# Eight three-slice products of state and w_in in place of twelve two-slice ones, and another output tile last, in a fused attention and snake kernel

## The chip, the cores and the metric

The kernel runs on one core of a Trainium2 chip. The metric is the device time of one execution in microseconds (us); the number compared is the median of several executions. TensorE (PE in the profile) does the matrix products and writes them to PSUM, which has eight banks here; ScalarE (ACT), VectorE (DVE) and GpSimd (POOL) do the elementwise work; SyncE (SP) issues most of the transfers.

## The reference

Two things are computed one after the other. First, for eight batches and eight heads, tokens read from a small state and the state reads from the tokens. Then every row that comes out goes through a two-matrix network with a snake activation.

```python
B, H, S, Ns, D = 8, 8, 512, 32, 64           # x: B,H,S,D; state: B,H,Ns,D
a  = softmax(x @ state.T / sqrt(D))          # over the 32 state slots
xread = a @ state                            # (B, H, 512, 64)
a2 = softmax(state @ x.T / sqrt(D))          # over the 512 tokens
sread = a2 @ x                               # (B, H, 32, 64)
rows = concat([xread, sread], axis=2)        # 8 * 544 = 4352 rows of 512 = H*D
h = rows @ w_in                              # 512 -> 2048
g = h + sin(alpha * h) ** 2 / (alpha + 1e-9)
out = g @ w_out                              # 2048 -> 512, float32
```

## The kernel before

The 4352 rows are handled as nine groups: group t = 0 to 7 holds the 512 ordinary tokens of batch t, and group t = 8 holds the 256 state reads of all batches together. Every group has 16 slices f of 128 columns of the 2048-wide hidden layer, and output tiles of 128 rows: four for an ordinary group, two for the state group.

For an ordinary batch the kernel does not form `xread` and then multiply it by `w_in`. It multiplies the state by `w_in` first: M = state times w_in, a table of 128 rows (four heads of 32 slots) by 2048 columns, for two head groups g. The hidden layer is then the attention weights AT times M, two matmuls for each slice f. The product for M is cut into four slices s of 512 columns. One slice takes eight matmuls which each use only a 64 by 32 piece of the array (`m`, L489), into two PSUM banks, one for each g. `me` (L497) copies a bank to M in SBUF as bf16; it runs on ACT or DVE. Slice s of M serves the hidden slices f = 4s to 4s+3.

The steps are small functions, and the string ORDER calls them one by one. Each engine works strictly in the order in which its own instructions stand there, so ORDER is the schedule, and it also names the PSUM bank of every product. The steps that matter here are:

- `lx`, `pk`, `td`: load x of a batch (POOL's queue), repack it (DVE), transpose it by DMA (SP's queue). `sc`, `ex`: the scores and their exponential. `rs`, `rr`, `nm`: row sums, reciprocals, normalised weights A (on POOL). `ad` (L441): the DMA transpose from A to AT, on SP's queue.
- `w` (L451), `cs` (L462), `rc`, `xs`: the state's read of a batch. The matmuls of `cs` use 64 columns of the array.
- `m` and `me`: the state times w_in, as above. `h` (L538, and L544 for the state group) and `hg` (L553): the hidden slice.
- `si` (L561), `sq` (L202 on POOL or DVE, L570 on ACT), `gt` (L577, DVE): sine, square, and the snake sum gT, which frees the bank of `h`.
- `o.t.st.f0.f1` (L588): matmuls f0 to f1 of an output tile; sixteen make a tile. `oc` (L596) copies the bank out, `os` (L603, or L606 for group 8) stores it on SP's queue. `oh`, `och` and `osh` are the same for a tile that is cut in 384 and 128 columns; the last tile is.

Before the change, M of batches 2 to 7 is made in twelve steps `m` of two slices, and each of them holds four banks. Batches 0 and 1 have eight slices at the start that are placed one or two at a time. The pool of M has two buffers. The tile that stands last in ORDER is the first one of the state group, `oh.8.0.0` and `oh.8.0.1`, right after `o.8.1`. Its store goes through this address pattern, whose outer dimension is the batch:

```python
ov = k.out.rearrange("(b t) c -> b t c", t=k.TB)
k.nc.sync.dma_start(ov[:, k.S + st::2, cols], o_sb[:, cols])
```

An ordinary tile is stored as 128 rows at a fixed step:

```python
k.nc.sync.dma_start(k.out[r0:r0 + k.C * (k.P - 1) + 1:k.C, cols], o_sb[:, cols])
```

Of the kernel before, what the change touches and what calls it, by code (L numbers as in the profile page):

```python
# [32 lines left out]
m.0.1.6.4 si.0.1 m.1.1.0.7 hg.0.3.0.2 me.1.1.1.A sq.0.2.V hg.0.3.1 sq.0.1.G me.1.1.0.V si.0.0  # L33
warm_up.2.128.7 gt.0.2 warm_up.2.128.7 me.0.1.1.A warm_up.2.128.0 sq.0.0.G warm_up.2.128.7
warm_up.2.128.0 me.0.1.0.A gt.0.1 m.1.2.7.1 si.0.3 m.0.2.4.0 hg.0.4.0.6 me.1.2.1.V me.1.2.0.A
hg.0.4.1 sq.0.3.G hg.0.6.0.5 me.0.2.0.V hg.0.6.1 si.0.4 hg.0.5.0.1 hg.0.5.1 me.0.2.1.V si.0.6
hg.0.11.0.7 sq.0.4.G hg.0.7.0.4 gt.0.0 hg.0.7.1 si.0.5 hg.0.11.1 hg.0.8.0.0 gt.0.3 hg.0.8.1 sq.0.6.A
sq.0.5.G o.0.0.0.2.3 si.0.11 gt.0.4 o.0.0.2.3 o.0.3.0.2.2 si.0.7 o.0.3.2.3 gt.0.6 sq.0.11.G
o.0.3.3.4 o.0.2.0.1.6 si.0.8 o.0.2.1.2 gt.0.5 o.0.3.4.5 sq.0.7.A o.0.2.2.3 sq.0.8.G o.0.2.3.4
gt.0.11 hg.0.9.0.5 hg.0.9.1 hg.0.10.0.1 gt.0.7 hg.0.10.1 si.0.9 o.0.2.4.6 gt.0.8 si.0.10 o.0.3.5.6  # L40
sq.0.9.G o.0.0.3.4 o.0.3.6.8 sq.0.10.A xt.1.1.7 pk.1.1.V pk.1.0.V xt.1.0.4 xc.1.1.1.A xc.1.1.0.V
o.0.0.4.5 gt.0.10 xc.1.0.1.A o.0.0.5.6 sc.1.1.0 xc.1.0.0.A o.0.0.6.7 gt.0.9 o.0.2.6.8 sc.1.0.7
m.0.3.1.4 ex.1.0 o.0.1.0.1.5 me.0.3.0.V o.0.1.1.4 me.0.3.1.V o.0.1.4.7 hg.0.13.0.1 o.0.1.7.8 ex.1.1
rs.1.0 hg.0.13.1 hg.0.12.0.4 o.0.2.8.9 si.0.13 rr.1.0 hg.0.12.1 rs.1.1 nm.1.0.0.4.G m.1.3.7.0
o.0.3.8.9 rr.1.1 o.0.3.9.10 me.1.3.1.V o.0.3.10.11 nm.1.1.0.4.G o.0.1.8.10 me.1.3.0.V si.0.12
o.0.1.10.12 o.0.0.7.8 sq.0.13.G ad.1 hg.0.15.0.0 sq.0.12.A o.0.0.8.9 hg.0.15.1 o.0.0.9.10 gt.0.12
o.0.0.10.11 si.0.15 hg.0.14.0.7 o.0.0.11.12 gt.0.13 hg.0.14.1 sq.0.15.A o.0.1.12.13 o.0.2.9.11
si.0.14 gt.0.15 o.0.3.11.14 sq.0.14.A o.0.0.12.13 pk.2.0.V o.0.1.13.14 pk.2.1.V h.1.2.4 gt.0.14
h.1.4.1 td.2 si.1.2 lx.3.0.1 h.1.0.0 si.1.4 o.0.0.13.15 sq.1.2.V h.1.1.7 si.1.0 gt.1.2 sq.1.4.G
o.0.3.14.16 si.1.1 o.0.2.11.13 sq.1.0.A oc.0.3.V h.1.3.4 sq.1.1.G gt.1.4 o.0.0.15.16 os.0.3 h.1.6.2  # L50
si.1.3 oc.0.0.V o.0.2.13.15 si.1.6 sq.1.3.G o.0.2.15.16 gt.1.1 h.1.13.1 os.0.0 oc.0.2.A o.0.1.14.15
gt.1.0 o.0.1.15.16 sq.1.6.G si.1.13 h.1.7.3 os.0.2 gt.1.3 oc.0.1.A h.1.5.7 sq.1.13.G h.1.15.6 si.1.7
gt.1.6 os.0.1 o.1.1.0.1.0 si.1.5 o.1.1.1.3 sq.1.7.G gt.1.13 o.1.1.3.4 si.1.15 h.1.8.5 h.1.9.4
sq.1.5.A sq.1.15.G gt.1.7 o.1.2.0.1.2 si.1.8 h.1.12.1 gt.1.5 o.1.2.1.2 si.1.9 o.1.2.2.3 sq.1.8.G
o.1.2.3.4 gt.1.15 h.1.10.3 si.1.12 o.1.2.4.5 sq.1.9.A pk.3.1.V o.1.2.5.6 sq.1.12.G gt.1.8 h.1.11.7
si.1.10 h.1.14.6 gt.1.9 o.1.1.4.5 si.1.11 sq.1.10.G o.1.2.6.7 sc.2.1.5 gt.1.12 si.1.14 o.1.2.7.9
o.1.1.5.6 sq.1.11.A pk.3.0.V o.1.1.6.7 sq.1.14.G gt.1.10 o.1.1.7.8 td.3 sc.2.0.4 o.1.3.0.1.1 gt.1.11
o.1.3.1.2 ex.2.0 o.1.1.8.10 gt.1.14 o.1.3.2.3 o.1.2.9.10 o.1.3.3.5 o.1.1.10.11 o.1.2.10.11 ex.2.1
o.1.2.11.12 rs.2.0 o.1.2.12.15 rr.2.0 o.1.2.15.16 rs.2.1 nm.2.0.0.4.G m.2.2.3.7.6.4 oc.1.2.A
o.1.3.5.6 rr.2.1 me.2.2.0.A me.2.2.1.V w.0.5 os.1.2 nm.2.1.0.4.G me.2.3.1.A o.1.3.6.7 me.2.3.0.V  # L60
cs.0 m.2.0.2.3.7.4 ad.2 rc.0 o.1.3.7.8 me.2.1.1.A o.1.3.8.9 sc.3.0.6 me.2.0.1.V me.2.1.0.A
o.1.3.9.11 me.2.0.0.A sc.3.1.4 xs.0.0 o.1.1.11.12 xs.0.1 o.1.1.12.13 ex.3.0 o.1.1.13.15 o.1.3.11.12
ex.3.1 rs.3.0 o.1.3.12.14 o.1.1.15.16 rr.3.0 h.2.0.3 rs.3.1 nm.3.0.0.4.G oc.1.1.A o.1.3.14.16 si.2.0
rr.3.1 h.2.9.7 os.1.1 nm.3.1.0.4.G oc.1.3.V o.1.0.0.1.2 h.2.2.5 os.1.3 h.2.1.6 lx.4.0.1 ad.3 h.2.3.4
si.2.9 o.1.0.1.3 sq.2.0.V si.2.1 o.1.0.3.4 sq.2.9.G gt.2.0 o.1.0.4.6 si.2.3 o.1.0.6.8 si.2.2
sq.2.1.G h.2.8.0 gt.2.9 h.2.4.1 sq.2.3.A o.2.3.0.1.3 sq.2.2.G o.1.0.8.9 gt.2.1 si.2.8 h.2.5.7 si.2.4
o.1.0.9.10 gt.2.3 o.1.0.10.11 sq.2.8.G o.1.0.11.12 si.2.5 h.2.7.6 gt.2.2 o.2.3.1.2 sq.2.4.A
o.1.0.12.13 sq.2.5.G gt.2.8 o.1.0.13.14 si.2.7 o.1.0.14.15 h.2.6.4 gt.2.4 h.2.14.5 sq.2.7.A gt.2.5
o.1.0.15.16 o.2.3.2.3 si.2.6 o.2.3.3.4 pk.4.0.V o.2.3.4.5 oc.1.0.A pk.4.1.V h.2.11.0 sq.2.6.G gt.2.7
si.2.14 h.2.12.1 td.4 h.2.10.7 si.2.11 sq.2.14.G o.2.0.0.1.2 gt.2.6 o.2.0.1.2 si.2.10 o.2.0.2.4  # L70
sq.2.11.A o.2.0.4.5 os.1.0 sq.2.10.V o.2.0.5.6 gt.2.14 h.2.15.6 si.2.12 o.2.3.5.6 gt.2.10 h.2.13.4
si.2.15 sq.2.12.G o.2.0.6.7 gt.2.11 o.2.3.6.7 si.2.13 o.2.3.7.9 sq.2.15.G o.2.3.9.10 gt.2.12
sq.2.13.A o.2.0.7.10 gt.2.13 o.2.0.10.11 sc.4.1.5 sc.4.0.7 gt.2.15 o.2.3.10.12 ex.4.0 o.2.3.12.13
o.2.0.11.12 w.1.0 cs.1 o.2.3.13.14 rc.1 o.2.3.14.15 ex.4.1 o.2.3.15.16 m.3.0.1.4.6.7 oc.2.3.A rs.4.0
o.2.0.12.13 me.3.0.1.A o.2.0.13.14 os.2.3 o.2.0.14.15 me.3.0.0.V me.3.1.1.A o.2.0.15.16 o.2.1.0.2.5
rr.4.0 oc.2.0.A rs.4.1 o.2.1.2.3 nm.4.0.0.4.G o.2.1.3.4 me.3.1.0.A h.3.1.3 os.2.0 rr.4.1 xs.1.1
m.3.2.4.1.7.2 si.3.1 nm.4.1.0.4.G xs.1.0 h.3.0.6 me.3.3.1.V h.3.2.0 ad.4 me.3.3.0.V o.2.1.4.6
lx.5.0.1 h.3.6.2 me.3.2.1.V si.3.2 o.2.2.0.2.7 sq.3.1.V si.3.0 o.2.2.2.3 sq.3.2.G me.3.2.0.V
h.3.14.1 si.3.6 o.2.2.3.4 gt.3.1 o.2.2.4.5 si.3.14 sq.3.0.G o.2.2.5.7 gt.3.2 o.2.2.7.8 sq.3.6.A
o.2.2.8.9 h.3.9.4 sq.3.14.G gt.3.0 h.3.8.3 si.3.9 gt.3.6 h.3.5.0 si.3.8 h.3.10.6 sq.3.9.G gt.3.14  # L80
o.2.2.9.10 si.3.5 o.2.2.10.13 si.3.10 sq.3.8.G gt.3.9 h.3.15.2 sq.3.5.A o.2.2.13.14 h.3.7.1
sq.3.10.G gt.3.8 si.3.15 o.2.2.14.15 o.2.1.6.7 h.3.4.4 si.3.7 gt.3.5 sq.3.15.G o.2.2.15.16 o.2.1.7.8
si.3.4 gt.3.10 o.2.1.8.10 sq.3.7.A o.2.1.10.11 gt.3.15 sq.3.4.G o.2.1.11.13 oc.2.2.A o.2.1.13.14
gt.3.7 o.2.1.14.16 os.2.2 h.3.12.3 gt.3.4 oc.2.1.A h.3.3.0 si.3.12 pk.5.0.V o.3.3.0.1.6 os.2.1
m.4.2.2.7.1.5 pk.5.1.V si.3.3 sq.3.12.V td.5 o.3.3.1.2 me.4.2.1.V me.4.3.1.A o.3.3.2.3 sq.3.3.G
o.3.2.0.1.4 me.4.3.0.A o.3.2.1.2 gt.3.12 o.3.2.2.3 h.3.11.5 me.4.2.0.A gt.3.3 h.4.12.7 si.3.11
h.4.9.1 si.4.12 h.4.10.3 sq.3.11.V o.3.3.3.4 si.4.9 gt.3.11 h.4.11.2 sq.4.12.G o.3.2.3.4 si.4.10
o.3.2.4.6 sq.4.9.A o.3.2.6.7 gt.4.12 sq.4.10.G o.3.2.7.9 si.4.11 o.3.2.9.10 gt.4.9 o.3.2.10.11
o.3.3.4.5 sq.4.11.A o.3.3.5.6 gt.4.10 o.3.3.6.8 m.4.0.0.5.7.1 gt.4.11 o.3.3.8.9 me.4.1.0.A
me.4.0.1.V h.3.13.3 me.4.0.0.A h.4.8.2 me.4.1.1.V h.4.15.7 si.3.13 h.4.2.5 si.4.8 sq.3.13.V  # L90
o.3.1.0.2.0 lx.6.0.1 si.4.15 gt.3.13 h.4.1.1 o.3.3.9.10 si.4.2 o.3.3.10.11 sq.4.15.V o.3.1.2.3
sq.4.8.G si.4.1 gt.4.15 o.3.1.3.4 o.3.3.11.13 sq.4.2.A h.4.13.3 sq.4.1.G gt.4.8 o.3.3.13.14 h.4.3.7
si.4.13 gt.4.2 o.3.2.11.12 o.3.3.14.15 si.4.3 sq.4.13.G o.3.3.15.16 gt.4.1 h.4.5.2 oc.3.3.A h.4.6.5
sq.4.3.G si.4.5 gt.4.13 o.3.2.12.13 os.3.3 o.3.0.0.1.1 si.4.6 h.4.14.6 sq.4.5.G o.3.2.13.14 gt.4.3
h.4.4.3 si.4.14 o.3.0.1.2 sq.4.6.A o.3.0.2.3 sq.4.14.G gt.4.5 o.3.0.3.4 h.4.0.7 si.4.4 gt.4.6
o.3.0.4.5 o.3.1.4.5 si.4.0 sq.4.4.G o.3.1.5.6 gt.4.14 w.2.2 sq.4.0.A o.3.2.14.16 pk.6.1.V o.3.1.6.7
gt.4.4 h.4.7.5 oc.3.2.A sc.5.0.6 pk.6.0.V os.3.2 si.4.7 o.3.1.7.8 gt.4.0 sc.5.1.4 td.6 o.3.0.5.7
ex.5.0 sq.4.7.G o.3.1.8.9 o.3.0.7.11 gt.4.7 o.3.0.11.12 o.3.1.9.10 o.3.0.12.13 o.3.1.10.11 ex.5.1
rs.5.0 cs.2 m.5.0.3.7.5.6 rs.5.1 o.4.3.0.1.4 me.5.1.1.A o.4.3.1.2 rr.5.0 o.3.1.11.12 me.5.0.1.V
me.5.1.0.A o.3.1.12.13 nm.5.0.0.4.G o.3.1.13.14 o.3.0.13.14 me.5.0.0.A rr.5.1 rc.2 o.3.0.14.16  # L100
nm.5.1.0.4.G o.4.3.2.4 oc.3.0.A m.6.0.6.5.7.3 xs.2.0 xs.2.1 os.3.0 o.4.3.4.5 me.6.0.1.A me.6.0.0.V
ad.5 o.4.3.5.6 sc.6.0.1 me.6.1.1.A sc.6.1.2 me.6.1.0.V o.3.1.14.15 w.3.5 ex.6.0 o.3.1.15.16 ex.6.1
rs.6.0 o.4.0.0.1.6 o.4.3.6.7 cs.3 oc.3.1.A rs.6.1 m.5.2.3.7.1.2 os.3.1 o.4.3.7.8 rr.6.0 me.5.3.1.A
me.5.2.1.V o.4.3.8.9 nm.6.0.0.4.G o.4.3.9.10 me.5.2.0.A o.4.2.0.1.0 rr.6.1 o.4.3.10.11 rc.3
# [560 lines left out]
```

## Time and profile before

| what | value |
|---|---|
| median of 3 runs | 225.24 us (225.04 to 225.65) |
| the profiled execution | 226.94 us |
| its span in the trace | 225.2 us |
| PE busy | 213.6 us, 95% |
| ACT, DVE, POOL busy | 173.4, 162.3, 112.3 us |
| matmuls of the output product, L588, 128x512 | 511, mean 379 ns (they overlap; one starts about every 216 ns) |
| matmuls of state times w_in, L489 | 256, mean 382 ns |
| copies of M, L497 | 34 on ACT of 593 ns, 30 on DVE of 678 ns |

The profiled execution took 1.74 us more than its span, and 1.70 us more than the median of the runs. In the rows of the profile a name such as `o_ps<-w_out_sb,gT` is output and inputs, `x14` a count, and brackets hold the idle time before an instruction and what ended it. A busy time of PE is modelled, since matmuls are pipelined.

### The profile page before, as it was taken

The numbers are of one execution on the slowest core, as the hardware profiler recorded it, in microseconds if no ns is written. First come the engines' busy times: TensorE is split into PE (matmuls) and PEld (weight loads), VectorE is DVE, ScalarE is ACT, GpSimd is POOL, SyncE is SP. The second block draws the span as 40 slices with busy tenths as digits, with TensorE's granted clock in tenths as the row PEclk, the third lists the DMA queues.
The fourth block names the chain that finished last, engine by engine and source line by source line (L and its number), as shares of the span: only waits on it lengthen the run. The fifth ranks groups of instructions, "written<-read, shape, count | busy, mean of one in ns | idle before, by whom it ended". The sixth has DMA issues, their size and how long they took to land.

```text
span 225.2 us, 4306 instructions
## 1 busy us (share of the span) xinstructions
PE 213.6 (95%) x1590; PEld 106.1 (47%) x1617; DVE 162.3 (72%) x282; ACT 173.4 (77%) x295; POOL 112.3 (50%) x121
## 2 busy tenths in 40 slices
PE   6999999999999899999999999999999999999990
PEld 2864544444544344444454344445445455565450
DVE  2579987899868989989888677876966987432220
ACT  4579878997799879998997889799849789574100
POOL 6957715695197338844843388396301366310000
PEclk9999999999999999999999999999999999999998
DMA  6999995944666629177244417710311100121213
GB/s 198 202 199 203 206 186 83 204 140 93 96 157 77 140 83 132 27 185 81 58 100 115 117 48 93 180 58 0 93 51 67 44 31 0 51 93 48 93 51 89
DMA packets 38045, 23.48 MB, mean 104 GB/s; under 512 B 20984, under 2 KB 33672, under 8 KB 38024
## 3 DMA queue, kind: packets, MB, share of 16 engines
q1 hardware_dynamic: 26120, 15.08, 25.9%
q0 software_dynamic: 11648, 8.13, 25.0%
q8 instruction: 12, 0.20, 0.3%
q14 instruction: 9, 0.07, 0.1%
q10 hardware_dynamic: 256, 0.01, 0.1%
HBM read 17.44 MB, written 8.91 MB: 117 GB/s over the span
## 4 chain that ended last, share of the span: by engine, by line
PE 80%; DMA 8%; DVE 4%; ACT 3%; issue 2%; POOL 1%; POOLq 0%
PE o_ps L588 45%; PE h_ps L538 18%; DMA xnat<-in_x_dram 4%; PE m_ps L489 3%; PE h_ps L544 3%; PE h_ps L553 3%; PE warm_ps L304 3%; DMA AT<-A 2%; DMA xT<-xp 2%; PE s_ps L400 2%; PE w_ps L451 1%; POOL A L202 1%; PE w_ps L462 1%; ACT M L497 1%; DVE gT L577 1%
## 5 line engine op out<-in xcount | busy, mean ns | idle before, releaser
L588 PE MATMUL o_ps<-w_out_sb,gT 128*128 128x512 bf16 (+2 forms) x543 | 135.0, 373 | 1.4 <-issue 0.6
L577 DVE SCALAR_TENSOR_TENSOR gT<-s,inva_sb,h_ps 128x512 bf16<-128x512 bf16 (+1 forms) x144 | 96.5, 712 | 23.6 <-ACT s L570 11.8
L202 POOL TENSOR_TENSOR s<-s 128x512 bf16<-128x512 bf16 (+1 forms) x82 | 82.0, 1015 | 57.2 <-ACT s L561 38.4
L561 ACT ACTIVATE s<-h_ps,alpha_sb 128x512 bf16<-128x512 f32 (+1 forms) x144 | 88.6, 670 | 10.4 <-PE h_ps L538 5.4
L588 PEld LDWEIGHTS <-gT 128*128 128x128 bf16 x560 | 52.2, 98 | 60.5 <-issue 5.0
L538 PE MATMUL h_ps<-AT,M 128*128 128x512 bf16 x216 | 59.4, 379 | 1.0 <-DVE gT L577 0.4
L538 PEld LDWEIGHTS <-M 128*128 128x128 bf16 x224 | 21.5, 98 | 27.4 <-issue 1.1
L570 ACT ACTIVATE s<-s 128x512 bf16<-128x512 bf16 (+1 forms) x51 | 30.3, 596 | 0.9
L202 POOL TENSOR_TENSOR A<-E,rR 128x512 bf16<-128x512 bf16 x16 | 16.5, 1047 | 28.6 <-DVE rR L417 10.3
L596 ACT COPY o_sb<-o_ps 128x512 f32<-128x512 f32 (+2 forms) x25 | 14.2, 568 | 20.3 <-PE o_ps L588 20.3
L497 ACT CAST M<-m_ps 128x512 bf16<-128x512 f32 x34 | 18.2, 593 | 6.6 <-PE m_ps L489 6.5
L497 DVE CAST M<-m_ps 128x512 bf16<-128x512 f32 x30 | 19.4, 678 | 2.2 <-PE m_ps L489 2.1
L596 DVE COPY o_sb<-o_ps 128x512 f32<-128x512 f32 x10 | 6.9, 689 | 12.2 <-PE o_ps L588 12.2
L411 DVE TENSOR_REDUCE R<-E 128x16 f32<-128x512 bf16 x16 | 10.4, 661 | 1.2 <-ACT E L407 1.1
L489 PE MATMUL m_ps<-w_in_sb,stT 64*32 64x512 bf16 x256 | 10.2, 382 | 0.0
L407 ACT ACTIVATE E<-s_ps 128x512 bf16<-128x512 f32 x16 | 8.9, 603 | 1.7 <-PE s_ps L400 1.6
L304 PE MATMUL warm_ps<-warm 128*128 128x128 bf16 (+1 forms) x64 | 7.9, 281 | 2.2 <-DVE warm L210 2.0
L202 DVE TENSOR_TENSOR s<-s 128x512 bf16<-128x512 bf16 x11 | 5.6, 513 | 5.6 <-ACT s L561 5.6
L469 DVE RECIPROCAL rC<-w_ps 128x128 f32<-128x128 f32 x8 | 7.5, 941 | 2.6 <-PE w_ps L462 2.4
L544 PE MATMUL h_ps<-xs_all,w_in_sb 128*128 128x256 bf16 x64 | 9.0, 273 | 0.0
L553 PE MATMUL h_ps<-AT,M 128*128 128x512 bf16 x30 | 8.3, 379 | 0.2 <-issue 0.2
L544 PEld LDWEIGHTS <-w_in_sb 128*128 128x128 bf16 x64 | 6.3, 98 | 3.1
(56 smaller groups left out, 106.8 us busy)
## 6 DMA issues: line engine op xcount, KB each, us to landing
out_dram<-o_sb SPq DMA_DIRECT2D x33, 256.0 KB, 2.2
xnat<-in_x_dram POOLq DMA_DIRECT2D x7, 512.0 KB, 7.6
w_in_sb<-in_moe_w_in_dram POOLq DMA_DIRECT2D x4, 512.0 KB, 10.0
w_out_sb<-in_moe_w_out_dram POOLq DMA_DIRECT2D x4, 512.0 KB, 16.2
x<-in_x_dram SPq DMA_DIRECT2D x4, 256.0 KB, 3.2
st_nat<-in_state_dram POOLq DMA_DIRECT2D x1, 256.0 KB, 5.1
out_dram<-o_sb SPq DMA_DIRECT2D x1, 192.0 KB
s<-in_state_dram SPq DMA_DIRECT2D x1, 128.0 KB, 2.2
```

The lines of the kernel that those rows point to most:

```text
L202: {"V": k.nc.vector, "G": k.nc.gpsimd}[eng].tensor_tensor(out, a, b, ALU.mult)
L304: k.nc.tensor.matmul(wp[:, :cols], k.warm[:, 0:k.P], k.warm[:, :cols], start=True, stop=True)
L489: k.nc.tensor.matmul(k.t["m", b, s + n, g][o0:o0 + k.Ns, :], k.stT[k.half(r), b * k.G + g, c0:c0 + k.Ns], k.w_in_sb[k.half(r), 2 * g + h, ...
L497: k.copy(eng)(k.t["M", b][:, g, s * k.FW:(s + 1) * k.FW], k.t["m", b, s, g][:])
L538: k.nc.tensor.matmul(hp[:, :n], k.t["M", t][:, g, fs], k.t["AT", t][:, g, :], start=(g == 0), stop=(g == k.G - 1),)
L544: k.nc.tensor.matmul(hp[:, :n], k.w_in_sb[:, q, fs], k.xs_all[:, q].rearrange("p b j -> p (b j)"), start=(q == 0), stop=(q == k.Q - 1),)
L553: k.nc.tensor.matmul(k.t["h", t, f][:], k.t["M", t][:, g, f * k.P:(f + 1) * k.P], k.t["AT", t][:, g, :], start=(g == 0), stop=(g == k.G - 1),)
L561: k.nc.scalar.activation(s[:, :n], k.t["h", t, f][:, :n], ACT.Sin, scale=k.alpha_sb[:, f:f + 1])
L570: k.nc.scalar.activation(s2[:, :n], s[:, :n], ACT.Square)
L577: k.nc.vector.scalar_tensor_tensor(gT[:, :n], k.t["s2", t, f][:, :n], k.inva_sb[:, f:f + 1], k.t["h", t, f][:, :n], ALU.mult, ALU.add,)
L588: k.nc.tensor.matmul(k.t["o", t, st, half][:, cols], k.t["gT", t, f][:, rows], k.w_out_sb[:, f, cols], start=(f == 0), stop=(f == k.FT - 1),)
L596: k.copy(eng)(o_sb[:, cols], k.t["o", t, st, half][:, cols])
```

## The change

The products for batches 2 to 7 are regrouped. A new step `mx.n` takes n pairs (batch, slice) and n pairs of banks, and calls `m` for each pair in turn without anything between. ORDER has eight of them with three slices each, so each fills six of the eight banks, and four of them mix two batches. M gets a third buffer. The two tiles of the state group leave the end of ORDER: they are now computed whole, before the last ordinary tile, and the tile cut in two is `7.3`, with `7.0` and `7.1` finished just before its second piece. Everything in ORDER after the products of slice 1 for batches 0 and 1 is laid out anew around this: the places of the steps, the banks, and which of ACT, DVE and POOL does a square, a copy or (once, `nm.4.1`) a normalisation. The work of each kind stays, but for six warm-up matmuls fewer at the start; `w_in` products of batches 0 and 1 now stand in six places instead of five.

```diff
-        k.mpool, k.epool, k.smallp = pool("mpool", 2), pool("epool", 4), pool("smallp", 4)
+        k.mpool, k.epool, k.smallp = pool("mpool", 3), pool("epool", 4), pool("smallp", 4)
...
+    def mx(k, n, *args):
+        for i in range(n):
+            k.m(*args[2 * i:2 * i + 2], *args[2 * n + 2 * i:2 * n + 2 * i + 2])
...
-o.1.2.11.12 rs.2.0 o.1.2.12.15 rr.2.0 o.1.2.15.16 rs.2.1 nm.2.0.0.4.G m.2.2.3.7.6.4 oc.1.2.A
-cs.0 m.2.0.2.3.7.4 ad.2 rc.0 o.1.3.7.8 me.2.1.1.A o.1.3.8.9 sc.3.0.6 me.2.0.1.V me.2.1.0.A
+oc.1.1.A mx.3.2.2.2.3.2.0.5.4.7.3.6.1 rr.2.1 oc.1.2.A os.1.1 nm.2.1.0.4.G w.0.0 os.1.2 me.2.0.0.A
+me.2.0.1.V sc.3.0.2 me.2.3.0.A cs.0 me.2.2.0.V ad.2 o.1.3.0.1.6 me.2.2.1.A rc.0 sc.3.1.1 me.2.3.1.A
+mx.3.2.1.3.0.3.1.7.5.4.3.2.0 rr.3.0 rs.3.1 o.1.3.8.9 nm.3.0.0.4.G me.3.1.0.A o.1.3.9.10 h.2.2.1
...
+mx.3.3.2.3.3.4.2.5.3.2.1.6.7 os.2.3 pk.5.0.V oc.2.0.A td.5 h.3.0.0 me.4.2.1.A me.3.3.0.V h.3.4.4
+o.3.3.1.3 oc.2.2.A o.3.3.3.4 gt.3.10 o.3.3.4.6 os.2.2 mx.3.4.3.4.0.4.1.4.2.1.6.5.7 o.3.2.0.1.3
+oc.3.0.A rr.5.0 mx.3.5.3.6.0.6.1.6.0.2.1.4.5 rs.5.1 nm.5.0.0.4.G os.3.0 o.4.3.0.1.7 rr.5.1
+me.5.3.1.A o.4.3.6.7 rc.2 ad.5 o.4.3.7.8 me.6.1.0.A o.4.3.8.11 xs.2.0 mx.3.5.0.5.1.5.2.5.2.1.6.0.4
+o.4.1.13.16 pk.7.1.V mx.3.6.2.6.3.7.2.5.0.6.4.7.1 pk.7.0.V oc.4.1.A td.7 h.5.6.3 me.7.2.1.V
+mx.3.7.3.7.0.7.1.2.5.0.6.4.3 rc.6 o.6.2.3.4 me.7.1.1.A o.6.2.4.5 me.7.0.0.V o.6.2.5.6 me.7.0.1.A
...
-o.7.2.6.16 oh.8.0.0.0 oc.7.2.V os.7.2 o.8.1.10.12 och.8.0.0.A o.8.1.12.14 osh.8.0.0 o.8.1.14.16
-oh.8.0.1.5 oc.8.1.V os.8.1 och.8.0.1.A osh.8.0.1
+o.7.0.7.9 oc.7.2.A o.8.0.0.3.5 os.7.2 o.8.0.3.16 o.7.0.9.11 oc.8.0.V o.8.1.0.3.3 os.8.0 o.8.1.3.16
+o.7.0.11.13 oc.8.1.A oh.7.3.0.0 os.8.1 o.7.1.12.14 och.7.3.0.A o.7.1.14.15 o.7.0.13.14 osh.7.3.0
+o.7.0.14.16 o.7.1.15.16 oh.7.3.1.4 oc.7.0.A oc.7.1.V os.7.0 os.7.1 och.7.3.1.A osh.7.3.1
```

In `mx.3.5.3.6.0.6.1.6.0.2.1.4.5`, for example, the slices are (batch 5, s 3), (6, 0) and (6, 1), and the banks are 6 and 0, 2 and 1, 4 and 5.

## The prediction

> **What bounds the kernel now.** I read the busy rows and slices first, then PE's waits, then PE's order of time around one product for M, then the end of the span.
>
> ```profile
> span 225.2 us, 4306 instructions
> PE 213.6 (95%) x1590; PEld 106.1 (47%) x1617; DVE 162.3 (72%) x282; ACT 173.4 (77%) x295; POOL 112.3 (50%) x121
> PE   6999999999999899999999999999999999999990
> ...
> PE 80%; DMA 8%; DVE 4%; ACT 3%; issue 2%; POOL 1%; POOLq 0%
> ```
>
> PE is full in every slice but the first and the last. A busy share can hide stalls, so the waits of PE come next.
>
> ```profile
> engine line waited for: us in total, times, longest us
> PE warm_ps L304 <- DVE warm L210: 2.0, 1, 2.0
> PE o_ps L588 <- issue: 0.6, 4, 0.2
> PE h_ps L538 <- DVE gT L577: 0.4, 1, 0.4
> ...
> PE s_ps L400 <- DMA xT<-xp: 0.4, 1, 0.4
> ...
> PE h_ps L538 <- DMA AT<-A: 0.3, 1, 0.3
> ```
>
> After the start, PE waits about 2 us in all. So a us taken out of PE's own stream counts in full, a us off another engine counts nothing, and every new wait of PE counts in full. The third view is PE in order of time around one two-slice product for M.
>
> ```profile
> 54.92 0.81 PE L588 MATMUL o_ps<-w_out_sb,gT 128*128 128x512 bf16 x3
> 55.66 0.63 PE L489 MATMUL m_ps<-w_in_sb,stT 64*32 64x512 bf16 x16
> 56.22 0.39 PE L588 MATMUL o_ps<-w_out_sb,gT 128*128 128x512 bf16 x1
> 56.45 0.63 PE L451 MATMUL w_ps<-E,xp 128*128 128x64 bf16 x16
> ```
>
> The last of the three L588 starts at 54.92 + 0.81 - 0.38 = 55.35, the next one at 56.22: 0.87 us apart, where two neighbours in a run are 0.216 apart. The step costs 0.655 us. The last view is the end: the slices and the stores of the state group.
>
> ```profile
> 217.20:219.60 2.40, 2.40 (x24) 1.47 (x21) 0.69 (x1) 0.48 (x1) 0.00 (x0) 1.00 0.06 11
> 219.60:221.00 1.40, 0.01 (x1) 0.00 (x0) 0.00 (x0) 0.27 (x1) 0.00 (x0) 1.00 0.44 125
> 221.00:222.00 1.00, 0.00 (x0) 0.00 (x0) 0.00 (x0) 0.00 (x0) 0.00 (x0) 1.00 0.45 70
> 222.00:223.00 1.00, 0.00 (x0) 0.00 (x0) 0.00 (x0) 0.00 (x0) 0.00 (x0) 1.00 0.49 163
> 223.00:224.00 1.00, 0.00 (x0) 0.00 (x0) 0.00 (x0) 0.00 (x0) 0.00 (x0) 0.52 0.28 91
> 224.00:225.20 1.20, 0.00 (x0) 0.00 (x0) 0.00 (x0) 0.00 (x0) 0.00 (x0) 0.50 0.00 0
> ```
>
> ```profile
> L603 SPq DMA_DIRECT2D out_dram<-o_sb x4: 332/332/333, 203.6 to 215.6; - x4
> L606 SPq DMA_DIRECT2D out_dram<-o_sb x3: 603/608/775, 218.0 to 220.2; - x3
> ```
>
> The columns after the stretch are sum, PE, PEld, DVE, ACT, POOL, granted clock, DMA share, GB/s. The last matmul ends at 219.63 and the span at 225.2: 5.57 us in which only the state group's stores run. They move 70 to 163 GB/s with under half of the DMA engines busy, until 224. They also take SP 603 to 775 ns each to issue, against 332 for an ordinary tile; the last issue starts at 220.18, because the one before it holds SP until 220.08.
>
> **The change, part by part.**
>
> *Fewer entries into the 64x32 form.* Eight of the twelve steps cost that (besides this one those at 80.85, 83.67, 96.20, 102.91, 121.27, 143.49 and 164.96, 0.65 to 0.66). Two slices stream 16 matmuls with eight in the array at once: 2 x 0.2155 = 0.431. So 0.224 is the price of going in and out. Single slices at the start support this: L489 x8 at 29.91 is followed after 0.35 us, x16 after 0.56, so one slice more is 0.21. Three slices then cost 0.224 + 0.647 = 0.87. Twelve by 0.655 is 7.86, eight by 0.87 is 6.96: 0.90 us less. Two corrections. Where `cs` stands directly before a product, both share one change of form: `cs` alone costs 0.445 (at 158.25), the pair at 118.10 costs 0.995 where 1.10 would be the sum. Before, four products have that neighbour (`cs` of 0, 2, 3 and 6), after only two (2 and 6): 0.2 back. And batches 0 and 1 enter six times instead of five: 0.2 back. Net -0.5 us. The page "TensorEngine Tiling", section "Tiling Modes", Key Properties, of the Trainium skill says that a change of mode drains the engine, without a price; the trace gives 0.224. Both ends: none of the entry is saved if the third slice brings a drain of its own (0), all of it without the corrections (-0.9).
>
> *Six banks held at once.* Three copies now fall to ACT or DVE after each product instead of two: 3 x 0.678 = 2.0 us on DVE, 3 x 0.593 = 1.8 on ACT, with two banks left to PE. The row first: after the two-slice products the next matmul waits at most 0.16 us, and it works in a bank that the product did not touch. Here a rule speaks against the change: the section "Performance Considerations", PSUM Bottleneck, of the same page says that tiling speeds up TensorE but not the evacuation, and that the copy may become the bottleneck. By the rule, with the third copy exposed each time, 8 x 0.64 = 5.1 us would be lost. By the row, the answer lies in what stands behind each `mx`. I walked the eight places with the durations of the rows. After the first: `w.0`, `sc.3.0` and `cs.0` (1.05 us) in banks of finished tiles, then bank 6, whose copy stands first on ACT. After the fifth: eleven matmuls of `o.4.3` in bank 7 (2.4 us), against 2.6 us until the last of the six copies, but its bank is wanted only by the third slice of the next product, another 0.5 us later. After the seventh: `h.5.6`, `h.5.7` in banks 3 and 2, then banks in the order in which they are copied. After the third I find two waits of about 0.2 us: `h.3.12` needs `me.3.3.1`, which stands behind `oc.2.0` and `me.4.2.1` on ACT, and `h.3.9` needs `me.3.2.1`, fourth on DVE behind `pk.5.0`. Behind a late copy stand that engine's next `si` or `gt`, and PE waits for these in turn. I take the row, +0.4 us, and keep -0.2 (a copy order that suits better than now) and +5.1 as ends.
>
> *The rest laid out anew.* PE, ACT, DVE and POOL have the same work: the copies of M move from 34 ACT, 30 DVE to 30 and 34, one `nm` goes from POOL to DVE (its 1.05 us there against about 0.5). ACT loads its function table as often (ten changes between sine and exponential in ORDER before and after; each 1.28 us). Between the second and third `mx` the ACT rows add up to 27.7 us and PE's to 27.2, so cover is thin there, yet before the same holds (22.2 against 21.8, 13.4 against 12.5) and PE waited only the times shown. The chain from `lx.4` to `sc.4` took 14.0 us before (63.82 to 77.85, with 0.36 of wait); in the new order `sc.4` comes about 14 us after `lx.4` too. `ad.2` has 4.1 us before (57.20 to 61.29), about 3.7 now, and the median from issue to landing is 3.9: about 0.2. At the start six warm-up matmuls (0.108 each, 0.65 us) go, but they only filled time: in the new order `m.0.2` waits for `me.1.1.0`, and `h.0.9` for `me.0.2.1`, about as long. I set this part at +0.2, with -0.8 and +1.5 as ends.
>
> *An ordinary tile last.* The last copy is the same (128x128 on ACT, 0.27 us). SP then issues in 0.33 instead of queueing behind 0.61 and taking 0.60. The stores of `7.0` and `7.1` (256 KB each) are issued just before: their matmuls end 1.1 us before the last one, their copies 0.6 and 0.35 before it. An ordinary store issued at 215.58 moved its data from about 216.4 to 217.15, at 370 to 420 GB/s, and lands 2.0 us after issue. So, counted from the last matmul T: data of both tiles from T+0.25 to T+1.65, the last 64 KB in 512 B pieces until about T+2.1. Between the last data (about 223.95) and the end of the span lie 1.25 us now; I add the same and get T+3.35, and take T+3.5, for a store issued at T+0.3 lands at T+2.3. That is 5.57 - 3.5 = 2.1 us less. The page "DMA: Bandwidth & Descriptors", section "Why a DMA increments its semaphore by 16 and not by 1", decides what the slow end is due to: a transfer uses the largest number up to 16 that divides both outer dimensions, 8 for the eight batches of the state store and 16 for 128 rows. The trace agrees with its shares, 0.44 to 0.49 here. If it were only the small last pieces, the gain would be the issue, about 0.7; by the page it is 2.1. I take 2.1, with 0.7 and 2.6 as ends. The state stores now leave about 8.5 and 4.8 us before T and are done before `7.0` needs the queue; they cost nothing as long as that cover holds, 1.3 us if the second ran into it.
>
> *The sum.* -0.5 + 0.4 + 0.2 - 2.1 = -2.0 us. The profiled execution would go from 226.94 to 224.9. It is 1.70 above the median; I take the same difference off the median: 225.24 - 2.0 = 223.2 us.
>
> **The rivals.**
>
> *The end is worth less.* Three stores, 768 KB with the 192 KB piece, crowd into the last 4 us; at 200 GB/s, the best that the state stores showed, 576 KB take 2.9 us and the gain is about 0.8. Then 223.2 + 1.3 = 224.5. Against it: ordinary stores alone ran at 370 to 420.
>
> *Slower: the third copy starves PE.* The place is behind `mx`, above all the third to the fourth and the fifth to the sixth, where hidden slices need M from copies that stand third on their engine. Each costs up to the 0.64 of one copy, and the delay goes on through `si`, `sq`, `gt` to the next bank. At 0.64 in all eight it is +5.1 instead of +0.4: 223.2 + 4.7 = 227.9. It decides from (2.0 + 0.4 + 0.7) / 8, about 0.4 us per product. For it: ACT's sums equal PE's in these stretches. Against it: copies of finished output tiles and a stock of gT give PE work in other banks at six of the eight.
>
> *It does not do what it says.* Each slice within `mx` could drain anew, since the banks of the next pair come free one by one. Then the product saves nothing, 223.2 + 0.9 = 224.1; the end still gains.
>
> **How the numbers follow.** About 0.3%, 0.7 us, is what a measurement of this kernel can tell from no change. Forecast case 0.64, own range 222.2 to 224.1; the end worth less 0.12, on the bound's edge, so half faster and half same; starved PE 0.16, nearly all slower; entries not saved 0.08, faster. Faster 0.77, same 0.08, slower 0.15. The range leaves out under 0.1 below and 0.1 above: 221.9 to 226.0.
>
> **What would show it.** The end: no L606 after the last matmul, and 3.2 to 3.8 us from the last matmul to the span's end instead of 5.57; a DMA share above 0.8 there. The products: L489 x24, and about 1.08 us from the L588 before to the one after; 1.3 or more says that it drains within. The banks: PE's waits on M copies and on gT together under 1.5 us after the start. The forecast is wrong if PE's busy share behind the third to sixth `mx` falls below 95%, if ACT or DVE is never idle there while PE waits, or if the state stores still run after the last matmul.

## The result, and the profile after

The changed kernel takes 223.19 us (median of four executions, 222.62 to 227.05) against 225.19 us for the kernel before: a ratio of 0.9899, 95% interval 0.9873 to 0.9925. Two later jobs on the chip gave 222.07 us (ratio 0.9851, 0.9821 to 0.9882) and 222.96 us (0.9893, 0.9866 to 0.9921). It is faster by 2.0 to 3.3 us in the medians; 223.2 us was forecast. Each job times the kernel before beside the others; executions slowed by a lower clock, such as the one at 227.05 us, are left out of the ratios.

The profiled execution of the changed kernel took 223.3 us. Its page, the busy rows and the slices of PE:

```profile
span 221.5 us, 4268 instructions
PE 212.7 (96%) x1585; PEld 106.7 (48%) x1611; DVE 165.5 (75%) x289; ACT 169.1 (76%) x289; POOL 110.7 (50%) x120
PE   6999999999989999999999999999999999999993
...
PE 92%; ACT 3%; DVE 2%; issue 1%; POOL 0%; POOLq 0%
```

PE is still what bounds it. The chain that ended last holds no step that waits for DMA; before it had 8% (a chain follows one releaser at each step, so this alone says little). The waits of PE from the first product for batches 2 to 7 (55.7 us) to the last matmul, with total, times and longest:

```profile
PE h_ps L537 <- ACT M L496: 0.6, 1, 0.6
PE o_ps L587 <- issue: 0.2, 1, 0.2
```

The same view of the kernel before, from 55.6 us on:

```profile
PE h_ps L538 <- DVE gT L577: 0.4, 1, 0.4
PE s_ps L400 <- DMA xT<-xp: 0.4, 1, 0.4
PE o_ps L588 <- issue: 0.3, 2, 0.2
PE h_ps L538 <- DMA AT<-A: 0.3, 1, 0.3
```

The rows on `issue` are most likely no waits. The traces of after_again, h2_later, end_apart and third_twice hold all 1611 matmuls and have no such row; the others hold 1585 or 1590 and have some, so a record is missing there. That goes for the "at most 0.16 us" which the prediction read off as a wait behind a product, too. The view also counts from the modelled end of a matmul, 0.38 us after its start, where neighbours start 0.216 apart: it leaves out the first 0.16 us of each wait. Without `issue`, 1.1 us of waits before and 0.6 after: the new layout has not brought new ones in sum. One product in the order of time of PE:

```profile
95.52 1.03 PE L587 MATMUL o_ps<-w_out_sb,gT 128*128 128x512 bf16 x4
96.47 0.84 PE L483 MATMUL m_ps<-w_in_sb,stT 64*32 64x512 bf16 x24
97.25 0.39 PE L587 MATMUL o_ps<-w_out_sb,gT 128*128 128x512 bf16 x1
```

The last of the four starts at 95.52 + 1.03 - 0.38 = 96.17, the next one at 97.25: 1.08 apart, so a three-slice product costs 0.87 us. The rows at 122.62 and 143.23 give the same. The end, by stretches (the columns as before: sum, PE, PEld, DVE, ACT, POOL, granted clock, DMA share, GB/s), and the stores from 205 us on:

```profile
217.20:218.06 0.86, 0.84 (x16) 0.67 (x12) 0.68 (x1) 0.36 (x1) 0.00 (x0) 1.00 0.44 159
218.06:219.00 0.94, 0.00 (x0) 0.00 (x0) 0.00 (x0) 0.27 (x1) 0.00 (x0) 1.00 0.61 231
219.00:220.00 1.00, 0.00 (x0) 0.00 (x0) 0.00 (x0) 0.00 (x0) 0.00 (x0) 1.00 0.99 355
220.00:221.00 1.00, 0.00 (x0) 0.00 (x0) 0.00 (x0) 0.00 (x0) 0.00 (x0) 1.00 0.07 18
```

```profile
L602 SPq DMA_DIRECT2D out_dram<-o_sb x5: 332/337/402, 205.5 to 218.5; - x5
L605 SPq DMA_DIRECT2D out_dram<-o_sb x2: 608/692/775, 209.5 to 213.3; - x2
```

The last matmul ends at 218.05 and the span at 221.5: 3.45 us, where it was 5.57. The DMA engines are busy to 0.99 from 219 to 220 us and move 355 GB/s, where the state stores had under half of them and 70 to 163 GB/s. Those (L605) are now issued at 209.5 and 213.3, beside matmuls.

So the two profiled executions differ by 3.64 us: about 2.1 at the end and 1.6 ahead of the last matmul (219.63 against 218.05). Both reach the first product for batches 2 to 7 at nearly the same time (55.66 and 55.77), so the 1.6 lies between it and the last matmul. The medians of that comparison differ by 2.0.

### The profile page after: what moved, and what is told of

Its sections match the earlier page's. It is cut to its first block, busy times and chain, and to the rows that moved or that the text cites. A ratio compares the mean times of both kernels' runs of the same rounds, so it can differ in the third digit from the quotient of the medians.

```text
span 221.5 us, 4268 instructions
## 1 busy us (share of the span) xinstructions
PE 212.7 (96%) x1585; PEld 106.7 (48%) x1611; DVE 165.5 (75%) x289; ACT 169.1 (76%) x289; POOL 110.7 (50%) x120
## 4 chain that ended last, share of the span: by engine, by line
PE 92%; ACT 3%; DVE 2%; issue 1%; POOL 0%; POOLq 0%
PE o_ps L587 52%; PE h_ps L537 22%; PE m_ps L483 3%; PE h_ps L552 3%; PE h_ps L543 3%; PE warm_ps L298 2%; PE s_ps L394 2%; PE w_ps L445 2%; PE w_ps L456 1%; ACT M L496 1%; ACT o_sb L595 1%; ACT xT L380 1%; POOL A L196 0%; PE x_ps L356 0%; PE st_ps L328 0%
## 5 line engine op out<-in xcount | busy, mean ns | idle before, releaser
L587 PE MATMUL o_ps<-w_out_sb,gT 128*128 128x512 bf16 (+2 forms) x541 | 131.8, 373 | 1.2 <-issue 0.3
L560 ACT ACTIVATE s<-h_ps,alpha_sb 128x512 bf16<-128x512 f32 (+1 forms) x144 | 87.6, 674 | 16.3 <-PE h_ps L537 8.9
L587 PEld LDWEIGHTS <-gT 128*128 128x128 bf16 x560 | 52.8, 98 | 60.6 <-issue 2.8
L569 ACT ACTIVATE s<-s 128x512 bf16<-128x512 bf16 (+1 forms) x51 | 31.1, 615 | 0.7
L196 POOL TENSOR_TENSOR A<-E,rR 128x512 bf16<-128x512 bf16 x15 | 15.6, 1049 | 27.7 <-DVE rR L411 11.5
L595 ACT COPY o_sb<-o_ps 128x512 f32<-128x512 f32 (+2 forms) x24 | 13.6, 574 | 16.9 <-PE o_ps L587 16.7
L496 DVE CAST M<-m_ps 128x512 bf16<-128x512 f32 x34 | 21.4, 677 | 3.8 <-PE m_ps L483 3.7
L496 ACT CAST M<-m_ps 128x512 bf16<-128x512 f32 x30 | 16.0, 595 | 5.2 <-PE m_ps L483 5.0
L595 DVE COPY o_sb<-o_ps 128x512 f32<-128x512 f32 x11 | 7.6, 688 | 15.6 <-PE o_ps L587 15.4
L483 PE MATMUL m_ps<-w_in_sb,stT 64*32 64x512 bf16 x256 | 9.6, 381 | 0.0
```

The costliest lines, as they stand in the source:

```text
L196: {"V": k.nc.vector, "G": k.nc.gpsimd}[eng].tensor_tensor(out, a, b, ALU.mult)
L483: k.nc.tensor.matmul(k.t["m", b, s + n, g][o0:o0 + k.Ns, :], k.stT[k.half(r), b * k.G + g, c0:c0 + k.Ns], k.w_in_sb[k.half(r), 2 * g + h, ...
L496: k.copy(eng)(k.t["M", b][:, g, s * k.FW:(s + 1) * k.FW], k.t["m", b, s, g][:])
L560: k.nc.scalar.activation(s[:, :n], k.t["h", t, f][:, :n], ACT.Sin, scale=k.alpha_sb[:, f:f + 1])
L569: k.nc.scalar.activation(s2[:, :n], s[:, :n], ACT.Square)
L587: k.nc.tensor.matmul(k.t["o", t, st, half][:, cols], k.t["gT", t, f][:, rows], k.w_out_sb[:, f, cols], start=(f == 0), stop=(f == k.FT - 1),)
```

## The experiments

The profiled execution of the kernel before stood 1.7 us above its median. Theory P holds that the end is worth about 2.1 us in ordinary executions too, Q that its end was unusually slow. The first four runs shared a job.

**tail_only: the end alone, in the kernel before.**

```diff
-o.7.2.0.1.2 o.8.1.4.5 oc.7.1.V o.7.2.1.4 os.7.1 o.8.1.5.6 o.7.2.4.5 o.8.1.6.7 o.7.2.5.6 o.8.1.7.10
-o.7.2.6.16 oh.8.0.0.0 oc.7.2.V os.7.2 o.8.1.10.12 och.8.0.0.A o.8.1.12.14 osh.8.0.0 o.8.1.14.16
-oh.8.0.1.5 oc.8.1.V os.8.1 och.8.0.1.A osh.8.0.1
+o.8.1.4.5 oc.7.1.V o.8.1.5.16 os.7.1 o.8.0.0.2.0 oc.8.1.V o.8.0.2.16 os.8.1 oh.7.2.0.2 oc.8.0.V os.8.0
+oh.7.2.1.5 och.7.2.0.A osh.7.2.0 och.7.2.1.A osh.7.2.1
```

> The kernel before with only its end changed: after the last matmuls of 7.1 the two state tiles are finished whole, and the ordinary tile 7.2 comes last in two pieces of 384 and 128 columns. Theory P, which the prediction holds: the end is worth 2.1 us, so 223.1 us, and the span ends about 3.4 us after the last matmul. Rival Q: the profiled execution of before, 1.7 us above its median, had an unusually slow end, and the end is worth 0.4 to 0.7 us in ordinary runs; then 224.6 us, and most of what the whole change gains lies in the middle.

Measured: 223.07 us against 225.05, ratio 0.9895 (0.9856 to 0.9935). The span ends 3.08 us after the last matmul (216.82 to 219.9). The end alone moves the median by 2.0 us, as P has it. In the trace the end is 2.5 us shorter than the 5.57 before.

**swap_rows: the address pattern alone.** The order and the sizes stay; only the destinations change places, in `os`, so those rows of the output come out exchanged:

```diff
         o_sb = k.t["o_sb", (t, st)]
+        if t == 7 and st >= 2:
+            t, st = 8, st - 2
+        elif t == 8:
+            t, st = 7, st + 2
         if t < k.B:
```

> The kernel before, with the destinations of tiles 7.2 and 7.3 exchanged with those of the two state tiles (their rows stand exchanged in the output); the order and the sizes are untouched, so the tile that is computed last is the same but leaves through the address pattern of 128 rows. If the slow end is due to the address pattern with 8 batches outermost: 0.33 us for each issue at the end, a DMA share near 0.9 after the last matmul, and the gain of the end as in tail_only (223.1 by P, 224.6 by Q). If it is due to small pieces being last: 225.2, no change.

Measured: 223.31 us against 225.05, ratio 0.9894 (0.9855 to 0.9934). The stores from 205 us on, and the stretches after the last matmul, which ended at 219.18:

```profile
L607 SPq DMA_DIRECT2D out_dram<-o_sb x5: 332/332/341, 207.0 to 219.5; - x5
L610 SPq DMA_DIRECT2D out_dram<-o_sb x1: 625/625/625, 215.1 to 215.1; - x1
```

```profile
219.17:220.00 0.83, 0.00 (x0) 0.00 (x0) 0.00 (x0) 0.27 (x1) 0.00 (x0) 1.00 0.17 65
220.00:221.00 1.00, 0.00 (x0) 0.00 (x0) 0.00 (x0) 0.00 (x0) 0.00 (x0) 1.00 0.80 279
221.00:222.30 1.30, 0.00 (x0) 0.00 (x0) 0.00 (x0) 0.00 (x0) 0.00 (x0) 1.00 0.00 0
```

The same tile computed last in the same pieces, but leaving as 128 rows (L607), ends 3.12 us after the last matmul instead of 5.57; the slow pattern (L610) is now used at 215.1, four us ahead of it. So the end's gain lies in the address pattern of what is stored last, not in small pieces or in which tile is computed last. In the traces the packets of the state stores at the end run mostly eight at a time, and those of 128-row stores reach sixteen; that agrees with the eight and sixteen engines which the prediction worked out.

**state_last: the end undone, in the changed kernel.**

```diff
-o.8.0.0.3.5 os.7.2 o.8.0.3.16 o.7.0.9.11 oc.8.0.V o.8.1.0.3.3 os.8.0 o.8.1.3.16 o.7.0.11.13 oc.8.1.A
-oh.7.3.0.0 os.8.1 o.7.1.12.14 och.7.3.0.A o.7.1.14.15 o.7.0.13.14 osh.7.3.0 o.7.0.14.16 o.7.1.15.16
-oh.7.3.1.4 oc.7.0.A oc.7.1.V os.7.0 os.7.1 och.7.3.1.A osh.7.3.1
+o.7.3.0.3.5 os.7.2 o.7.3.3.16 o.7.0.9.11 oc.7.3.V o.8.1.0.1.3 os.7.3 o.8.1.1.10 o.7.1.12.16
+o.7.0.11.16 oc.7.1.A os.7.1 oh.8.0.0.0 oc.7.0.V os.7.0 o.8.1.10.12 och.8.0.0.A o.8.1.12.14 osh.8.0.0
+o.8.1.14.16 oh.8.0.1.4 oc.8.1.V os.8.1 och.8.0.1.A osh.8.0.1
```

> The changed kernel with its end undone: 7.3 whole, 7.1 and 7.0 finished, and the state group last (8.1 and the two pieces of 8.0), as before the change; everything up to the last 13 us is the changed kernel's. Theory P: 223.1 + 2.1 = 225.2 us, so the regrouped middle is worth nothing. Rival Q: 223.6 us, the middle is worth about 1.5 us, as the two profiled executions have it (the last matmul at 218.06 against 219.63).

Measured: 225.13 us against 225.05 in the medians, ratio 0.9977 (0.9948 to 1.0006). The end is 5.63 us long again, with three stores of 603 to 780 ns on SP:

```profile
L605 SPq DMA_DIRECT2D out_dram<-o_sb x3: 603/608/780, 214.7 to 216.9; - x3
```

So by the ratio the regrouped middle is worth between 1.2 us and nothing, and the median is the one of theory P. The traces say more. From the start of the first product for batches 2 to 7 (the same work stands ahead of it in both orders, but for the warm-ups) to the last matmul, with the waits that the view shows in this stretch, `issue` left out:

| kernel | order up to the end | us | waits of PE, us |
|---|---|---|---|
| before | before | 163.97 | gT 0.4, xT 0.4, AT 0.3 |
| swap_rows | before | 163.58 | gT 0.5, xT 0.5 |
| tail_only | before | 162.81 | AT 0.4 |
| the changed kernel | after | 162.28 | first slice of batch 2 0.6 |
| after_again | after | 162.27 | the same 0.6 |
| after_third | after | 162.34 | the same 0.7 |
| state_last | after | 162.20 | the same 0.5 |
| end_apart | after | 161.99 | the same 0.3 |
| end_apart_2 | after | 162.75 | the same 0.2, xT 0.3 |

The old order took 162.8 to 164.0, the new one 162.0 to 162.8, and within each order the waits follow the spread. tail_only and state_last wait about equally long, 0.4 and 0.5, and differ by 0.6: about what the fewer entries were to save in this stretch (0.7). The rest of the difference to the first profile is waits that the old order has in two of its three traces.

The times agree with this once they are sorted. The twelve executions of state_last form two groups, five from 223.65 to 224.18 us and seven from 225.09 to 226.07; of the kernel before, nineteen lie from 224.32 to 225.67 and four from 226.18 to 227.09. The profiled execution of state_last (223.84) had an early start, that of the kernel before (226.94) a late one, as the last section tells. If the groups are the two starts, which only the profiled executions show, the medians of the lower groups differ by 1.2 us and those of the upper by 1.4. So the middle is worth about what rival Q says, and the whole change more than 2.0 us where the starts are alike.

**split_third: sixteen entries in place of eight.** For the first of them:

```diff
-mx.3.2.2.2.3.2.0.5.4.7.3.6.1 ... w.0.0 ... me.2.0.0.A
+mx.2.2.2.2.3.5.4.7.3 ... w.0.0 m.2.0.6.1 ... me.2.0.0.A
```

> The changed kernel with every mx cut: two slices, then one matmul or step of the ordinary kind that stood behind, then the third slice. Sixteen entries into the 64x32 form in place of eight, nothing else moved. By the price of 0.224 us for an entry: 8 x 0.224 = 1.8 us slower than the changed kernel, 224.9 us. If an entry inside a busy stream costs nothing and the saving comes from the new places of the steps: 223.1 us. If the six banks at once are what costs, the cut would make it faster, below 223.

Measured: 225.15 us, 2.0 us above the changed kernel's 223.19; against the kernel before of its job a ratio of 0.9987 (0.9960 to 1.0014). From the first product to the last matmul it took 164.90 us, 2.6 more. One of the cut products:

```profile
122.27 2.11 PE L587 MATMUL o_ps<-w_out_sb,gT 128*128 128x512 bf16 x9 [0.16 <-issue]
124.31 0.62 PE L483 MATMUL m_ps<-w_in_sb,stT 64*32 64x512 bf16 x16
124.86 0.39 PE L587 MATMUL o_ps<-w_out_sb,gT 128*128 128x512 bf16 x1
125.19 0.41 PE L483 MATMUL m_ps<-w_in_sb,stT 64*32 64x512 bf16 x8
125.53 0.39 PE L587 MATMUL o_ps<-w_out_sb,gT 128*128 128x512 bf16 x1
```

The last of the nine L587 starts at 122.27 + 2.11 - 0.38 = 124.00, the second one after it at 125.53: 1.53 us, of which 0.43 belong to two ordinary matmuls. That is 1.10 for three slices in two entries, where one entry took 0.87: 0.23 for the second. The cut product at 59.81 gives the same. An entry inside a busy stream has its price, and it is the 0.224 of the prediction. Eight of them make 1.9 of the 2.6 us; the rest, by the trace, is longer waits elsewhere, such as 0.3 us for the transposed x of batch 4.

The second four runs shared a job too.

**after_again: the changed kernel once more.** No edit.

> The changed kernel as it is, once more, as the mark for the other three on the same chip. 223.1 us; from the start of the first mx to the last matmul 162.3 us as in its first profile (the kernel before took 162.8 to 164.0 for the stretch from the same place in three profiles), and 3.44 us from the last matmul to the end.

Measured: 222.07 us, ratio 0.9851 (0.9821 to 0.9882); 162.27 us and 3.44 us for the two stretches. The stretches repeat to 0.02 us, while the profiled execution took 222.07 us instead of 223.3. The difference lies ahead of the first product, which starts at 54.59 instead of 55.77; the last section comes back to it.

**h2_later: cover for the one large wait.**

```diff
-... o.1.3.9.10 h.2.2.1 ... o.1.3.10.11 ... h.2.11.2 ... o.1.3.11.12 ... o.1.3.12.14
+... o.1.3.9.13 h.2.2.1 ... h.2.11.2 ... o.1.3.13.14
```

> The changed kernel with three matmuls of the output tile 1.3 moved ahead of the first hidden slice of batch 2, which in the changed kernel's profile waits 0.60 us with the transposed weights AT landing last. If AT is what it waits for (issue at 57.37, about 4 us to landing): the wait goes, 0.4 to 0.6 us faster, 222.6. If the copies of M on ACT are the releaser, as the matmul's own row has it, the same three matmuls hide it too, but the slices behind then wait for the next copies, and 0 to 0.2 us are gained.

The wait that it aims at, in after_again:

```profile
60.52 0.60 PE L537 MATMUL h_ps<-AT,M 128*128 128x512 bf16 x2 [0.56 <-DMA AT<-A]
```

Measured: 222.13 us against 222.07, and 162.53 us for the middle instead of 162.27. The wait is gone, but nothing was gained. What its waits have new is 0.3 us for the transposed x of batch 4:

```profile
PE s_ps L394 <- DMA xT<-xp: 0.3, 1, 0.3
```

Set side by side matmul by matmul (both traces are complete), h2_later is 0.73 us ahead after the first slice of batch 2 and loses 1.0 us between 70 and 76 us: 0.1 to 0.2 ahead of three hidden slices and 0.45 at this wait. So PE's wait moved to later places. end_apart_2, without this edit, has a short wait at the first slice (0.2) and the 0.3 for xT as well. Whether AT or the copy that ends beside it was the releaser stays open, since the edit covers both.

**end_apart: only the cut tile in flight at the end.**

```diff
-o.7.0.9.11 oc.8.0.V o.8.1.0.3.3 os.8.0 o.8.1.3.16 o.7.0.11.13 oc.8.1.A oh.7.3.0.0 os.8.1 ... osh.7.3.1
+o.7.0.9.16 oc.8.0.V o.8.1.0.3.3 os.8.0 oc.7.0.A os.7.0 o.8.1.3.16 o.7.1.12.16 oc.8.1.A os.8.1 oc.7.1.V
+os.7.1 oh.7.3.0.0 oh.7.3.1.4 och.7.3.0.A osh.7.3.0 och.7.3.1.A osh.7.3.1
```

> The changed kernel with 7.0 and 7.1 finished and stored before the cut tile 7.3 begins, so that only its own two pieces are in flight after the last matmul. Theory P: what stands in the end of the changed kernel is partly the queue of 576 KB; alone the last piece lands 2.0 us after its issue, as in tail_only, whose end was 3.07 us: 0.3 to 0.4 us faster, 222.8. Rival: the end is latency alone, which no order changes: 223.1 and still 3.4 us.

Measured: 221.87 us against 222.07 (ratio to before 0.9837, 0.9807 to 0.9867). The last matmul ends at 217.75, the span at 220.7: 2.95 us.

```profile
218.00:219.00 1.00, 0.00 (x0) 0.00 (x0) 0.00 (x0) 0.04 (x1) 0.00 (x0) 1.00 0.69 243
219.00:220.00 1.00, 0.00 (x0) 0.00 (x0) 0.00 (x0) 0.00 (x0) 0.00 (x0) 1.00 0.19 54
```

Counted from the last matmul, the last data is moved after 1.7 us; in after_again it is 2.1, with about 1.3 us more until the end of the span in both. So 0.4 to 0.5 us of the changed kernel's end was the queue of 7.0 and 7.1. The median shows less than that, so the pair was run again, as after_third and end_apart_2.

> The changed kernel a third time, as the mark for the next one: 222.1 to 223.2 us, 3.44 us from the last matmul to the end.

> The changed kernel with 7.0 and 7.1 finished and stored before the cut tile, a second time, to set its gain against the spread of the start. Its end was 2.95 us against 3.44: 0.5 us faster than the changed kernel of the same job. If its lead of 0.2 us in the medians was chance: the same within 0.2.

Measured: 222.96 and 222.01 us (ratios to before 0.9893, 0.9866 to 0.9921, and 0.9865, 0.9837 to 0.9892). The end was 3.4 us (218.37 to 221.8) and 2.95 (218.45 to 221.4). In the medians end_apart leads by 0.2 and by 0.95 us, and the intervals overlap, so the times alone don't settle it; the end itself is 0.45 to 0.5 us shorter in both pairs.

**third_twice: one more copy on each engine behind every mx.** For the first:

```diff
-me.2.0.0.A me.2.0.1.V
+me.2.0.0.A me.2.0.0.A me.2.0.1.V me.2.0.1.V
```

> The changed kernel with the two copies of the third slice of every mx made twice, 16 copies more (about 5 us of ACT and 5 of DVE in all). The prediction holds that the copies lie beside PE's work with some tenths of slack: one more on each engine takes 0.6 us there and about 0.2 to 0.4 of it reaches PE, 224 to 226 us. If the copies already bind behind every mx, all of it reaches PE: 8 x 0.64 = 5.1 us, 228. If there is ample slack: 223.1 to 223.6.

Measured: 225.27 us, 3.2 above after_again of the same job; 165.47 us from the first product to the last matmul, 3.2 more than 162.27. The waits of PE in that stretch:

```profile
PE o_ps L590 <- ACT M L499: 0.5, 2, 0.4
PE s_ps L397 <- DMA xT<-xp: 0.3, 1, 0.3
PE h_ps L540 <- DMA AT<-A: 0.2, 1, 0.2
PE m_ps L486 <- ACT M L499: 0.2, 1, 0.2
PE h_ps L540 <- ACT M L499: 0.2, 1, 0.2
```

Copies of M now release PE in the view, but only for 0.9 us of the 3.2. The rest is in waits that the view cuts short: matmul by matmul against after_again, the first slice of batch 2 waits 0.35 us less, and thirteen other places take 0.08 to 0.55 us more, 3.5 in sum. About 0.9 of these stand at the same places as in h2_later (70 to 77 us), which has no added copies. So of the added 0.64 us per product 0.3 to 0.4 reaches the end, as expected, and the slack behind the third copy is some 0.2 to 0.3 us on average, not ample.

## Why the prediction was right or wrong

*The median: right, but in part by luck.* 223.19 measured for 223.2, and faster as forecast. For the profiled execution the same sum gave 224.9, and 223.3 was measured, 1.6 us lower. Most of that is the waits of the middle, which came out about 1.4 us better than forecast. The step that made up for it is the last of the sum, which took the 1.70 us between the profile and the median of the kernel before off the changed kernel too: its own profile stood only 0.1 above its median in that job. The 1.70 is most likely a late start of one execution, not a property of the kernel. In the two later jobs the gain was 3.3 and 2.3 us.

*An ordinary tile last: right in size and cause.* -2.1 forecast, -2.12 in the profile, -2.0 by tail_only; T+3.5 forecast, T+3.45 measured, with 0.33 us for an issue and no state store after the last matmul. The choice of the address pattern as cause, which rested on the Trainium skill's page "DMA: Bandwidth & Descriptors", section "Why a DMA increments its semaphore by 16 and not by 1", is shown by swap_rows. The parts are right too: the last data at T+2.1 as forecast, with the queue of 7.0 and 7.1 in it, and 1.35 us from there to the end where 1.25 was taken.

*Fewer entries: right.* 0.87 us for a three-slice product, as worked out. split_third confirms that the price is one of entering and leaving, 0.23 us. The rival by which each slice drains anew is excluded by the rows of 24.

*Six banks held at once: mis-signed.* +0.4 was taken for new waits, with two of 0.2 us behind the third `mx`. No such wait stands in the profile: PE waits once for 0.6, at the first slice of batch 2, which I had at 0.2 under the transfer of AT. The rule of the Trainium skill's page "TensorEngine Tiling", section "Performance Considerations", PSUM Bottleneck, by which the copies out of PSUM may become what binds, did not decide here, since six copies of 0.6 to 0.68 us fitted; but third_twice shows that it is near: 0.2 to 0.3 us of slack for each product.

*The rest laid out anew: mis-signed too.* +0.2 forecast. The waits for gT and xT which stand in the profile before (0.4 each) are absent from that of the changed kernel, and its one wait is longer than the AT wait before. I walked only the new places where a wait could arise, and took the old waits to come back as they were. In sum the view has 0.5 us less of waits, about 0.8 with the first 0.16 us of each, where the two terms said 0.6 more; with the entries' share after the first product (-0.9 and 0.2 back) this gives 1.5 of the 1.7 us between the first product and the last matmul. It isn't a fixed gain: tail_only has the old order without the waits for gT and xT, and end_apart_2 the new order with one for xT. Why they come and go was not tried.

*The range* of 221.9 to 226.0 held the first job's median, and 222.07 and 222.96 of the two later ones, the first of them only just.

*The slower rival:* its place was right: with an added copy behind each product, third_twice lost 3.2 us, 0.4 per product, which is its decision point, and the kernel was back at 225.27 against 225.38. The change itself stays on the near side of it.

## What to carry to other kernels

Look first at what runs after the last instruction of the bounding engine: here stores with under half of the DMA engines busy, 5.57 us long. A store of 128 rows put last in place of one with eight batches outermost took 2 us off at no cost elsewhere that the runs show. Regrouping work that changes the array's form saves a fixed time for each entry left out, here 0.23 us; count the copies that follow, and try how much slack they have by making one of them twice. When an order is laid out anew, count the old order's waits as removable before you add new ones. And when one profiled execution stands off the median, find out in which stretch before you take the difference over to another kernel.

## What the runs showed of the hardware

The start is not the same in each execution. PE and weight loads by stretch, and ten warm-up matmuls of 128 columns, first in the kernel before and then in tail_only, which have the same order there:

```profile
8.80:10.30 1.50, 1.50 (x21) 1.41 (x18) 1.27 (x3) 0.32 (x1) 1.32 (x2) 1.00 1.24 206
8.64 1.27 PE L304 MATMUL warm_ps<-warm 128*128 128x128 bf16 x10
```

```profile
8.80:10.30 1.50, 1.50 (x47) 1.36 (x44) 1.01 (x3) 1.24 (x4) 1.50 (x3) 1.00 1.23 197
8.15 0.72 PE L303 MATMUL warm_ps<-warm 128*128 128x128 bf16 x10
```

In 1.5 us PE starts 21 matmuls in the one and 47 in the other, and the warm-ups start 107 ns apart in the one and 56 in the other. The slow pace lasts until 11.4 us in the first; in the second it is last seen at 6.6, and the full pace from 7.4 on. The first product for batch 2 then starts at 55.66 and at 54.01.

The column of the granted clock reads 1.00 in both, since it counts time without a record as full. The record itself tells more: in the trace of the kernel before it begins at 11.4 us, just where the pace changes (tail_only has none). In the other ten traces it begins at 5.2 to 11.1 us. It lasts 211.6, 215.0 or 218.5 us before half the clock is granted, so it differs by steps of 3.41 us. The page "TensorE: Matmul & The Clock Gate" of the Trainium skill, section "Part 1: The HAM clock gate", says that the clock is released after about 3.4 us of activity counted in a window that runs freely, so that the moment depends on where a kernel starts in it. The steps agree with that window. The page gives the variation as 500 ns either way, and the one measured here is wider, some 6 us.

An early clock is not all of it: split_third has the full pace from 5.4 us on and its first product at 55.53, and its PE waits 0.8 us for the load of the state and 0.5 for the weights at the start. A start that varies by 1 to 2 us would explain most of the spread between executions of one kernel, and why stretches measured from a fixed place in the order repeat better than times. That most executions of the kernel before had an early start and its profile a late one is likely by this, but only one trace of it exists.
